# One change in four parts to a fused attention and two-layer kernel: where a rounding runs, how input splits are queued, how fast operands are fetched, how long one weight group is prepared

## The chip, the cores and the metric

The kernel runs on one core of a Trainium2 chip. The metric is the device time of one execution in microseconds. The engines are named as in the profile: PE is TensorE (PEld its weight loads), DVE is VectorE, ACT is ScalarE, POOL is GpSimd, and SP is SyncE, which here issues nearly all the DMAs. Each engine runs its own instructions strictly in the order in which the program emitted them, so an instruction that waits holds up everything behind it on that engine.

## The reference, cut to what matters

```python
def phi(x):                                   # w_phi: 64 x 128
    proj = x @ w_phi
    proj = proj - max(abs(proj))              # over the features
    return concat([exp(proj), exp(-proj)])
num, den = phi(q) @ (phi(k).T @ v), phi(q) @ sum(phi(k))
x = num / (den + 1e-6)                        # 4 batches, 8 heads, 576 tokens, 64 wide
x = x as 2304 tokens x 512
h = x @ w_in;   g = h / (1 + exp(-h));  x = g @ w_out    # 512 -> 2048 -> 512
h = x @ w2_in;  g = h * cos(h);         out = g @ w2_out # 512 -> 2048 -> 512
```

The four weight matrices arrive as 64-bit floats. Products are made to nearly full fp32 accuracy by splitting every operand into a rounded high part and a remainder (hi and lo) and adding three products of parts.

## The kernel before, in words

Attention comes first and ends at about 200 us of the profile. Then come the two layers, and the change lies almost wholly there.

**Blocks, groups and steps.** The 2304 tokens are four blocks of 512 (0 to 3) and a small rest ("S"). The 2048 inner features are four groups g = 0 to 3 of 512. A step treats one block with one group: `step` computes h by a Strassen-like scheme of seven products (p 1 to 7, at L778, each against one of seven weight operands A11, S1, A12, S2, S4, S3, A22), applies the nonlinearity (`act`), and multiplies by w_out (`y`, L844 to L851, with four further weight operands 0 to 3). For each layer the order is: groups 0 to 3 over blocks 0, 1, S, and then groups 0 to 3 again over blocks 2 and 3. A step has seven calls of `fill()` (a small step has four), and each call adds one to a counter, `weights.now`. One such unit is about 3 us of PE work. All hand-made scheduling is in these units: `at[layer, g, block]` is the unit at which a step starts.

**The nonlinearity of the second layer** (`act`) is h * cos(h), in pieces of 128x512. Each piece passes through three stages that `begin` and `advance` emit at fixed places of a step: ACT computes the angle in turns, a = h / 2pi + 1/4 (L811). Then `turns`: DVE rounds a to the nearest integer by adding and subtracting 12582912 in one tensor_scalar (L802), DVE subtracts (L803), ACT takes the sine (L804). Then `times`: three DVE instructions multiply by h and split into gh and gl (L807 to L809). A full step has four such pieces; there are 72 in all. In a step, ACT also makes the copies of product banks at L959, L965 and L973, for which PE waits before it goes on with those banks.

**Input splits** (`Inputs.build`). Before a block can be used, its four quarter blocks and four differences T1 to T4 are split into hi and lo: `split` puts ACT's copy to hi (L613) and DVE's subtraction for lo (L614) next to each other as one task. Blocks that come back from memory are read by four load tasks of two DMAs each (L598) into the places where the lo parts will lie, so a lo may be written only when the differences that read that raw block are done. The differences of these blocks run on POOL (L607). Each list of tasks is spread over a stretch of units.

**Weight operands.** `in_tasks` and `out_tasks` turn 64-bit weights into fp32 with ACT (L169) and DVE (L170, L175, L181), add them on POOL (L235), and split them on ACT and POOL (L189, L192). All operands are also stored to memory, and from the step (0, 3, 1) on they are fetched again when needed (L131). For the groups of the second layer, the (1, g), this preparation runs ahead and only stores. There are 16 slots of 512 KB, 11 of which a group uses. `fill()` runs `loads()`, which fetches the next wanted operands as long as slots are free; while preparation tasks are left it keeps two slots (SPARE) back. If a step needs an operand that was not fetched, `need` forces it at that place.

Of the kernel before, what the change touches and what calls it, by code (L numbers as in the profile page):

```python
# [7 lines left out]
F32 = mybir.dt.float32  # L8
F32R = mybir.dt.float32r
I32 = mybir.dt.int32  # L10
AF = mybir.ActivationFunctionType
ALU = mybir.AluOpType
# [3 lines left out]
P = 128  # L16
# [17 lines left out]
PB, T2, KN = 2, 2, 2  # L34
# [5 lines left out]
MAGIC = 12582912.0  # L40
INV2PI = 1.0 / (2.0 * math.pi)
# [3 lines left out]
SMALL = "S"  # L45
# [29 lines left out]
class Weights:  # L75
# [53 lines left out]
    def load(self, l, g, n):  # L129
        t = self.slot()  # L130
        self.nc.sync.dma_start(t.bitcast(F32), self.dram[l, g, n])  # L131
        self.have[l, g, n] = t
# [53 lines left out]
    def split(self, t, hi, lo):  # L186
        nc = self.nc
        if self.fast:
            nc.scalar.copy(hi, t)  # L189
        else:  # L190
            nc.gpsimd.tensor_scalar(hi, t, 1.0, 0.0, op0=ALU.mult, op1=ALU.add)
        nc.gpsimd.tensor_sub(lo, t, hi.bitcast(F32))  # L192
# [375 lines left out]
class Inputs:  # L568
# [11 lines left out]
    def build(self, tag, temps, dram=None):  # L580

        nc, i = self.nc, tag[1] % 2
        o = self.ops[i]
        tmp = {}
        where = {"11": 0, "12": 1, "21": 2, "22": 3}

        def block(n):
            kh, th = int(n[0]) - 1, int(n[1]) - 1
            if dram is None:
                return self.xa[:, NJ * i + 2 * th:NJ * i + 2 * th + 2, 2 * kh:2 * kh + 2, :].rearrange("p i c n -> p c i n")  # L590
            return o[:, 1, where[n]].bitcast(F32).rearrange("p c (i n) -> p c i n", n=P)

        def load(n):
            def go():
                kh, th = int(n[0]) - 1, int(n[1]) - 1
                src = dram.rearrange("p (i c n) -> p c i n", i=NJ, c=NC)[:, 2 * kh:2 * kh + 2, 2 * th:2 * th + 2, :]
                for c in range(2):
                    nc.sync.dma_start(block(n)[:, c], src[:, c])  # L598
            return go

        def part(n):
            return tmp[n].rearrange("p (c i n) -> p c i n", c=2, i=2) if n[0] == "T" else block(n)

        def diff(n, a, b, engine):
            def go():
                tmp[n] = temps()
                engine.tensor_sub(part(n), part(a), part(b))  # L607
            return go

        def split(n, idx):  # L610
            def go():
                hi, lo = (o[:, x, idx].rearrange("p c (i n) -> p c i n", n=P) for x in range(2))
                nc.scalar.copy(hi, part(n))  # L613
                nc.vector.tensor_sub(lo, part(n), hi.bitcast(F32))  # L614
                tmp.pop(n, None)
                self.done.add((tag, idx))
            return go

        d, g = nc.vector if dram is None else nc.gpsimd, nc.gpsimd
        out = [] if dram is None else [load(n) for n in ("11", "21", "22", "12")]  # L620
        t1 = diff("T1", "12", "11", d)
        if out:
            after(out[-1], 3, t1)
        return out + [t1, split("11", 0), diff("T2", "22", "T1", d), split("T1", 4),
                      diff("T4", "21", "T2", g), split("21", 2), split("T2", 5), diff("T3", "22", "12", g),
                      split("22", 3), split("T3", 6), split("T4", 1)]

    def build_small(self, tag, temps):
        nc = self.nc
# [22 lines left out]
def after(other, lag, f):  # L652

    f.after = (other, lag)
    return f
# [53 lines left out]
def moe(tc, xa, xd, yd, inputs, norm, norm_pool, weights, tasks, out):  # L709
    nc = tc.nc  # L710
    with ExitStack() as ctx:
        sp = ctx.enter_context(tc.tile_pool(name="mo", bufs=1, side="right", reuse_waits="tile"))
# [3 lines left out]
        inputs.add(sp, 1)  # L716
        quarter = sp.tile([P, 1], F32, name="quarter")
        nc.gpsimd.memset(quarter, 0.25)

        def temps():  # L720
            return weights.pool.tile([P, 2 * TH], F32, name="tt", bufs=2)
# [5 lines left out]
        at = {}  # L727
        n = 0
# [13 lines left out]
        def loads(forced=False):  # L742
            least = 0 if forced or not (tasks.streams.get("in") or tasks.streams.get("out")) else SPARE
            while wanted and opened[0]:
                key = wanted[0]
                if forced:
                    if key in weights.have or key not in weights.saved or not weights.free:
                        return
                    weights.load(*key)
                else:  # L750
                    if key in weights.have or weights.now < weights.saved.get(key, 1e9) + 2 or weights.slots() <= least:
                        return
                    weights.load(*key)
                wanted.pop(0)

        def need(l, g, n):
            key = (l, g, n)
# [31 lines left out]
        def act(s, part, at, h):  # L789

            hi, lo = (t[:, :, at] for t in tile_g(s, part))
            a = sp.tile([P, 2, TH], F32, name="ta", bufs=2)
            if s[0] == 0:
                def silu():
                    nc.scalar.activation(a, h, AF.Silu)
                    nc.scalar.copy(hi, a)  # L796

                return [silu, lambda: nc.vector.tensor_sub(lo, a, hi.bitcast(F32))]  # L798
            b = sp.tile([P, 2, TH], F32, name="tb", bufs=2)

            def turns():
                nc.vector.tensor_scalar(b, a, MAGIC, MAGIC, op0=ALU.add, op1=ALU.subtract)  # L802
                nc.vector.tensor_sub(b, a, b)  # L803
                nc.scalar.activation(b, b, AF.Sin, scale=2.0 * math.pi)  # L804

            def times():
                nc.vector.tensor_mul(b, b, h)  # L807
                nc.vector.tensor_copy(hi, b)  # L808
                nc.vector.tensor_sub(lo, b, hi.bitcast(F32))  # L809

            return [lambda: nc.scalar.activation(a, h, AF.Identity, bias=quarter, scale=INV2PI), turns, times]  # L811

        late = []

# [206 lines left out]
        def queue(l, g):  # L1021
            for kind, q in weights.order.items():
                q.extend((kind, l, GF * g + c) for c in range(GF))

        def plan():
            w = weights
            for l, g in [(0, g) for g in range(1, NG)] + [(1, g) for g in range(NG)]:
                ins, outs = w.in_tasks(l, g, (l, g) not in STORED), w.out_tasks(l, g, (l, g) not in STORED)
                queue(l, g)
                if (l, g) in STORED:  # L1030
                    a, b = at[0, NG - 1, 0] + 2, at[0, NG - 1, 3] + 2
                    ends = (a + (b - a) * g / 3, a + (b - a) * (g + 1) / 3) if g < 3 else (at[1, 0, SMALL], at[1, 2, 0])
                    tasks.add("in", ins, *ends)
                    tasks.add("out", outs, *ends)
                    continue
                b0, b1, bs, nx = at[l, g - 1, 0], at[l, g - 1, 1], at[l, g - 1, SMALL], at[l, g, 0]
                tasks.add("in", ins[:12], *((b0 + 1, b1 - 1) if (l, g) != (0, 1) else (b0 + 6, b1 + 3)))
                tasks.add("in", ins[12:21], b1 - 1, b1 + 6)
                tasks.add("in", ins[21:], b1 + 6, bs + 3)
                tasks.add("out", outs[:3], b1, b1 + 6)  # L1040
                tasks.add("out", outs[3:], bs + 1, nx + 6.5)
            b = inputs.build((0, 1), temps)
            tasks.add("build1", b[:2], 0, 0)
            tasks.add("build1", b[2:], 3, 7)
            l = NG - 1
            for tag, src, used, start in (((0, 2), xd[2], at[0, l, 0], at[0, l, 1] + 2),
                                               ((0, 3), xd[3], at[0, l, 1], at[0, l, SMALL] + 2),
                                               ((1, 0), yd[0], at[0, l, 2], at[0, l, 3] + 1),
                                               ((1, 1), yd[1], at[0, l, 3], at[1, 0, 0]),
                                               ((1, 2), yd[2], at[1, l, 0], at[1, l, 1] + 2),  # L1050
                                               ((1, 3), yd[3], at[1, l, 1], at[1, l, SMALL] + 2)):
                b = inputs.build(tag, temps, src)
                name = f"build{tag[1] % 2}"
                for f, d in zip(b, (1, 3, 4, 6)):
                    tasks.add(name, [f], used + d, used + d)
                tasks.add(name, b[4:], start, start + 8)
            for n, t in enumerate((at[0, 0, 1] + 2, at[0, 0, 3])):
                tasks.add("buildS", inputs.build_small((n, SMALL), temps), t, t + 5)

# [10 lines left out]
        for i, s in enumerate(steps):  # L1070
            layer, g, blk, _ = s
# [100 lines left out]
```

## Time and profile before

| what | value |
|---|---|
| time of the runs | 1027.44 us median of 3 (1024.21 to 1027.95) |
| time of the profiled execution | 1014.94 us |
| its span | 1013.2 us |
| mean granted TensorE clock | 0.987 |

The profiled execution is one execution, and it is 12.5 us shorter than the median of the runs. In the views below a time in the span counts from its start; a busy time is followed by the number of instructions as (x36); "idle before" is time that an engine stood still directly ahead of an instruction, with the instruction that ended it behind an arrow. The second layer begins at about 597 us.

### The profile page before, as it was taken

How to read it: one execution, taken by the hardware profiler on the slowest of the kernel's cores; microseconds unless marked ns; L12 is line 12 of the kernel's file. 1: busy time of each engine (PE TensorE's matmuls, PEld its weight loads, DVE VectorE, ACT ScalarE, POOL GpSimd, SP SyncE). 2: the span in 40 equal slices, each digit the busy share in tenths (PEclk: the TensorE clock that was granted, in tenths of full speed). 3: DMA queues.
4: the chain of work that ended last, by engine and by line, in shares of the span. 5: the costliest groups of instructions: out<-in, count | busy, mean ns of one | idle time of the engine just before them, and what ended most of it. 6: DMA issues, size and time to landing. Idle time of an engine off the chain costs nothing.

```text
span 1013.2 us, 16847 instructions
## 1 busy us (share of the span) xinstructions
PE 968.4 (96%) x6503; PEld 868.3 (86%) x6503; DVE 711.7 (70%) x1045; ACT 491.3 (48%) x918; POOL 279.9 (28%) x251
## 2 busy tenths in 40 slices
PE   8899999989999999989999998999899998999998
PEld 8799988878889998978899877888789877888897
DVE  6668787796756656875555558689876877667766
ACT  5666666765654454465544534452332334443331
POOL 2222554464361522740612621014200121000000
PEclk9999999999999999999999999999999999999999
DMA  5455446265754548878788785243635273443302
GB/s 158 141 136 143 115 139 176 67 234 185 254 204 164 202 165 289 307 301 319 279 305 307 265 298 169 105 172 137 240 135 166 84 260 113 147 161 110 126 1 83
DMA packets 97888, 186.46 MB, mean 184 GB/s; under 512 B 30352, under 2 KB 59152, under 8 KB 97040
## 3 DMA queue, kind: packets, MB, share of 16 engines
q1 hardware_dynamic: 97664, 185.25, 53.8%
q8 instruction: 51, 0.84, 0.3%
q14 instruction: 29, 0.24, 0.1%
q10 hardware_dynamic: 144, 0.13, 0.0%
HBM read 128.06 MB, written 57.22 MB: 183 GB/s over the span
## 4 chain that ended last, share of the span: by engine, by line
PE 69%; DVE 14%; ACT 5%; DMA 4%; POOL 4%; issue 3%; SPq 0%; DVEq 0%; ACTq 0%; POOLq 0%
PE h L778 27%; PE y L844 5%; PE y L845 5%; PE y L846 5%; PE y L851 5%; PE y L849 5%; PE y L850 5%; PE kv L473 3%; PE p L393 3%; PE num L499 2%; DVE tb L803 2%; DVE xa L879 2%; DVE gl L809 1%; DVE xo L614 1%; DVE tb L807 1%
## 5 line engine op out<-in xcount | busy, mean ns | idle before, releaser
L778 PEld LDWEIGHTS h<-xo,w 128*128 128x128 f32 x2688 | 331.7, 189 | 28.0 <-ACT h L959 8.7
L778 PE MATMUL h<-xo,w 128*128 128x256 f32 x2688 | 337.4, 282 | 17.3 <-ACT h L959 7.5
L804 ACT ACTIVATE tb<-tb 128x512 f32<-128x512 f32 x72 | 45.5, 632 | 177.6 <-DVE tb L803 177.2
L844 PE MATMUL y<-gh,w 128*128 128x512 f32 (+1 forms) x320 | 120.7, 377 | 4.6 <-DVE xa L879 3.3
L849 PE MATMUL y<-w,gh 128*128 128x512 f32 x288 | 116.0, 403 | 7.4 <-DVE gh L808 6.5
L845 PE MATMUL y<-gl,w 128*128 128x512 f32 (+1 forms) x320 | 119.9, 375 | 0.5 <-DVE gl L798 0.5
L846 PE MATMUL y<-gh,w 128*128 128x512 f32 (+1 forms) x320 | 119.4, 373 | 0.0
L851 PE MATMUL y<-w,gl 128*128 128x512 f32 x288 | 116.3, 404 | 0.9 <-DVE gl L809 0.9
L850 PE MATMUL y<-w,gh 128*128 128x512 f32 x288 | 115.6, 401 | 0.0
L192 POOL TENSOR_TENSOR w<-wt,w 128x512 fp32r<-128x512 f32 x32 | 45.5, 1422 | 207.3 <-ACT w L189 180.4
L798 DVE TENSOR_TENSOR gl<-ta,gh 128x512 fp32r<-128x512 f32 x72 | 64.3, 894 | 53.6 <-ACT gh L796 53.5
L192 POOL TENSOR_TENSOR w<-stage,w 128x512 fp32r<-128x512 f32 x56 | 79.3, 1425 | 66.6 <-ACT w L189 63.1
L879 DVE TENSOR_TENSOR xa<-y,xa 128x512 f32<-128x512 f32 (+1 forms) x114 | 69.7, 654 | 23.6 <-PE y L846 18.9
L844 PEld LDWEIGHTS y<-gh,w 128*128 128x128 f32 x320 | 60.5, 189 | 15.5 <-DVE xa L879 4.4
L849 PEld LDWEIGHTS y<-w,gh 128*128 128x128 f32 x288 | 55.4, 192 | 19.6 <-DVE gh L808 7.9
L846 PEld LDWEIGHTS y<-gh,w 128*128 128x128 f32 x320 | 60.6, 189 | 11.9 <-POOL w L192 0.2
L845 PEld LDWEIGHTS y<-gl,w 128*128 128x128 f32 x320 | 60.6, 189 | 10.4 <-DVE gl L798 0.8
L851 PEld LDWEIGHTS y<-w,gl 128*128 128x128 f32 x288 | 55.3, 192 | 15.4 <-DVE gl L809 2.2
L473 PE MATMUL kv<-va,kp 128*128 128x65 f32 x512 | 64.7, 270 | 0.2 <-ACT kp L415 0.2
L850 PEld LDWEIGHTS y<-w,gh 128*128 128x128 f32 x288 | 55.3, 192 | 10.8
L473 PEld LDWEIGHTS kv<-va,kp 128*128 128x128 f32 x512 | 62.7, 193 | 0.4 <-ACT kp L415 0.4
L802 DVE TENSOR_SCALAR tb<-ta 128x512 f32<-128x512 f32 x72 | 34.0, 472 | 36.6 <-ACT ta L811 36.6
(115 smaller groups left out, 1621.2 us busy)
## 6 DMA issues: line engine op xcount, KB each, us to landing
w<-d SPq DMA_DIRECT2D x48, 512.0 KB, 5.8
raw_in<-in_moe_w_in SPq DMA_DIRECT2D x32, 512.0 KB, 4.6
raw_out<-in_moe_w_out SPq DMA_DIRECT2D x32, 512.0 KB, 4.5
d<-w SPq DMA_DIRECT2D x32, 512.0 KB, 4.3
rb<-rd SPq DMA_DIRECT2D x16, 288.0 KB, 3.7
va<-in_v SPq DMA_DIRECT2D x32, 128.0 KB, 5.2
yd<-xa SPq DMA_DIRECT2D x4, 1024.0 KB, 4.2
xo<-yd SPq DMA_DIRECT2D x32, 128.0 KB, 5.0
```

What stands on the lines that cost most here:

```text
L192: nc.gpsimd.tensor_sub(lo, t, hi.bitcast(F32))
L473: nc.tensor.matmul(ps[:, c, x, :], kp[n, 1 + 2 * p + x][:, c, j, :], va[:, p + 2 * x, j, :], start=False, stop=(x == 1 and j == NJ - 1))
L778: nc.tensor.matmul(dst[:, ab], w[:, a, ab, c * P:(c + 1) * P], o[:, b, idx, c], start=start and n == 1, stop=n == 12, skip_group_check=True)
L798: return [silu, lambda: nc.vector.tensor_sub(lo, a, hi.bitcast(F32))]
L804: nc.scalar.activation(b, b, AF.Sin, scale=2.0 * math.pi)
L844: nc.tensor.matmul(o, w[:, 0, at], hi[:, f, x], stop=False, **st)
L845: nc.tensor.matmul(o, w[:, 0, at], lo[:, f, x], start=False, stop=False)
L846: nc.tensor.matmul(o, w[:, 1, at], hi[:, f, x], start=False, stop=en)
L849: nc.tensor.matmul(o, hi[:, f, at], w[:, 0], stop=False, **st)
L850: nc.tensor.matmul(o, hi[:, f, at], w[:, 1], start=False, stop=False)
L851: nc.tensor.matmul(o, lo[:, f, at], w[:, 0], start=False, stop=en)
L879: nc.vector.tensor_tensor(v, o, v, op=ALU.add)
```

## The change

1. **Rounding of the second layer.** `angle` now emits two ACT instructions: the angle a as before, and b = a + 12582912 (Identity with a bias tile `magic`). `turns` has one DVE instruction, b = (b - 12582912) - a, a scalar_tensor_tensor, in place of two, and ACT takes the sine with the sign turned.
2. **Input splits.** `split` gives two tasks, `high` (ACT) and `low` (DVE), and a low may come at the earliest one unit after its high. The list has 18 tasks behind the loads in place of 11, with the highs ahead of the lows in groups of two. T1 waits four units for the last load in place of three. The tasks behind the loads are spread over seven units in place of eight; for block (0, 1) the stretch ends at unit 8 in place of 7. Block (0, 0) keeps each pair together.
3. **Fetches.** A call of `loads` that is not forced returns after one fetch.
4. **The group (1, 3)** is prepared over the units at[1, 0, S] to at[1, 2, S] in place of at[1, 0, S] to at[1, 2, 0], which is 36 units in place of 22.

```diff
         def split(n, idx):
...
+            def high():
                 nc.scalar.copy(hi, part(n))
+
+            def low():
                 nc.vector.tensor_sub(lo, part(n), hi.bitcast(F32))
                 tmp.pop(n, None)
                 self.done.add((tag, idx))
-            return go
+
+            return high, after(high, 1, low)
...
-        if out:
-            after(out[-1], 3, t1)
-        return out + [t1, split("11", 0), diff("T2", "22", "T1", d), split("T1", 4),
-                      diff("T4", "21", "T2", g), split("21", 2), split("T2", 5), diff("T3", "22", "12", g),
-                      split("22", 3), split("T3", 6), split("T4", 1)]
+        if loads:
+            after(loads[-1], 4, t1)
...
+        return loads + [t1, h0, t2, h4, l0, l4, t4, h2, h5, l2, l5, t3, h3, h6, l3, l6, h1, l1]
...
+        magic = sp.tile([P, 1], F32, name="magic")
+        nc.gpsimd.memset(magic, MAGIC)
...
                 wanted.pop(0)
+                if not forced:
+                    return
...
-                nc.vector.tensor_scalar(b, a, MAGIC, MAGIC, op0=ALU.add, op1=ALU.subtract)
-                nc.vector.tensor_sub(b, a, b)
-                nc.scalar.activation(b, b, AF.Sin, scale=2.0 * math.pi)
+                nc.vector.scalar_tensor_tensor(b, b, MAGIC, a, op0=ALU.subtract, op1=ALU.subtract)
+                nc.scalar.activation(b, b, AF.Sin, scale=-2.0 * math.pi)
...
-            return [lambda: nc.scalar.activation(a, h, AF.Identity, bias=quarter, scale=INV2PI), turns, times]
+            def angle():
+                nc.scalar.activation(a, h, AF.Identity, bias=quarter, scale=INV2PI)
+                nc.scalar.activation(b, a, AF.Identity, bias=magic)
+
+            return [angle, turns, times]
...
-                    ends = (a + (b - a) * g / 3, a + (b - a) * (g + 1) / 3) if g < 3 else (at[1, 0, SMALL], at[1, 2, 0])
+                    ends = (a + (b - a) * g / 3, a + (b - a) * (g + 1) / 3) if g < 3 else (at[1, 0, SMALL], at[1, 2, SMALL])
...
-            tasks.add("build1", b[2:], 3, 7)
+            tasks.add("build1", b[2:], 3, 8)
...
-                tasks.add(name, b[4:], start, start + 8)
+                tasks.add(name, b[4:], start, start + 7)
```

## Rows read from the trace of the kernel before

**Rows 1.** The page: busy time of each engine, with its share of the span.
```profile
PE 968.4 (96%) x6503; PEld 868.3 (86%) x6503; DVE 711.7 (70%) x1045; ACT 491.3 (48%) x918; POOL 279.9 (28%) x251
```
**Rows 2.** Busy time by stretch: length, PE, PEld, DVE, ACT, POOL, clock, DMA share, GB/s.
```profile
380.00:445.00 65.00, 60.00 (x391) 53.87 (x389) 49.98 (x66) 32.67 (x58) 34.28 (x23) 1.00 0.81 288
600.00:630.00 30.00, 23.94 (x138) 21.04 (x137) 22.87 (x37) 11.13 (x20) 5.31 (x4) 0.94 0.52 178
665.00:720.00 55.00, 48.19 (x276) 41.32 (x276) 51.73 (x71) 20.26 (x36) 17.47 (x13) 0.97 0.35 128
720.00:780.00 60.00, 60.00 (x390) 54.48 (x390) 40.38 (x69) 19.74 (x32) 2.55 (x2) 1.00 0.59 202
780.00:865.00 85.00, 78.01 (x465) 67.83 (x464) 66.88 (x106) 30.66 (x52) 11.40 (x8) 0.96 0.48 154
```
**Rows 3.** Waits of PE, 230 to 870 us: total, times, longest.
```profile
PE h L778 <- ACT h L959: 6.9, 4, 2.7
PE y L849 <- DVE gh L808: 6.5, 3, 3.1
```
**Rows 4.** Timeline, 598 to 626 us: start, length, engine, instruction, idle before.
```profile
603.63 1.30 POOL L607 TENSOR_TENSOR tt<-xo 128x512 f32<-128x512 f32 x1 [11.39 <-DMA xo<-yd]
...
604.97 0.69 DVE L614 TENSOR_TENSOR xo<-xo 128x512 fp32r<-128x512 f32 x1 [3.56 <-POOL tt L607]
...
608.33 0.63 ACT L804 ACTIVATE tb<-tb 128x512 f32<-128x512 f32 x1 [7.06 <-DVE tb L803]
...
609.00 2.90 PE L778 MATMUL h<-xo,w 128*128 128x256 f32 x12 [3.31 <-ACT tb L804]
...
623.22 2.98 PE L778 MATMUL h<-xo,w 128*128 128x256 f32 x23 [2.74 <-ACT h L959]
```
**Rows 5.** Busy time in two 2 us stretches behind stalls of PE.
```profile
610.00:612.00 2.00, 2.00 (x10) 2.00 (x10) 1.97 (x5) 0.22 (x1) 0.00 (x0) 0.50 0.00 0
...
828.00:830.00 2.00, 2.00 (x6) 1.61 (x5) 1.54 (x3) 0.40 (x1) 0.00 (x0) 0.50 0.63 234
```
**Rows 6.** DVE's groups, 665 to 720 us: busy, mean ns, idle before.
```profile
L803 DVE TENSOR_TENSOR tb<-ta,tb 128x512 f32<-128x512 f32 x9 | 6.2, 692 | 0.3
L802 DVE TENSOR_SCALAR tb<-ta 128x512 f32<-128x512 f32 x9 | 5.9, 660 | 0.0
...
L175 DVE SCALAR_TENSOR_TENSOR wt<-raw_out,wt 128x512 int32<-128x512 int32 x3 | 4.3, 1418 | 0.0
...
L181 DVE SCALAR_TENSOR_TENSOR wt<-ws,wt 128x512 int32<-128x512 int32 x3 | 2.1, 684 | 0.0
```
**Rows 7.** DVE's busy time, 665 to 720 us, on tile wt, then on tile stage.
```profile
665.00:720.00 55.00, 7.57 (x9) 0.97 0.35 128
...
665.00:720.00 55.00, 3.58 (x6) 0.97 0.35 128
```
**Rows 8.** The page's costliest groups, by form, whole span: ACT's angle from SBUF.
```profile
L811 ACT ACTIVATE ta<-u,quarter 128x512 f32<-128x512 f32 x32 | 23.1, 723 | 19.3 <-DVE u L979 12.1 <-DVE u L992 7.1
```
**Rows 9.** SP's timeline, 520 to 600 us: DMA issues near the end of layer one.
```profile
591.86 1.59 SPq L131 DMA_DIRECT2D w<-d  x3
593.95 1.72 SPq L598 DMA_DIRECT2D xo<-yd  x2
```
**Rows 10.** DVE's groups, 780 to 865 us.
```profile
L802 DVE TENSOR_SCALAR tb<-ta 128x512 f32<-128x512 f32 x14 | 7.2, 512 | 1.7 <-ACT ta L811 1.7
...
L614 DVE TENSOR_TENSOR xo<-tt,xo 128x512 fp32r<-128x512 f32 x8 | 5.5, 688 | 6.4 <-ACT xo L613 6.4
...
L614 DVE TENSOR_TENSOR xo<-xo 128x512 fp32r<-128x512 f32 x6 | 4.1, 688 | 3.8 <-ACT xo L613 3.8
```
**Rows 11.** DVE's groups, 380 to 445 us.
```profile
L614 DVE TENSOR_TENSOR xo<-xo 128x512 fp32r<-128x512 f32 x6 | 6.9, 1154 | 5.2 <-issue 2.1 <-POOL stage L235 1.9 <-POOL tt L607 1.2
...
L614 DVE TENSOR_TENSOR xo<-tt,xo 128x512 fp32r<-128x512 f32 x7 | 6.2, 893 | 2.9 <-ACT xo L613 2.9
```
**Rows 12.** The page's DMA issues: KB each, median us from issue to landing.
```profile
w<-d SPq DMA_DIRECT2D x48, 512.0 KB, 5.8
```

More of the change, by code (lines that the diff above doesn't have):

```diff
@@ L610, in split @@
         def split(n, idx):
-            def go():
-                hi, lo = (o[:, x, idx].rearrange("p c (i n) -> p c i n", n=P) for x in range(2))
+            hi, lo = (o[:, x, idx].rearrange("p c (i n) -> p c i n", n=P) for x in range(2))
+            def high():
                 nc.scalar.copy(hi, part(n))
+            def low():
                 nc.vector.tensor_sub(lo, part(n), hi.bitcast(F32))
@@ L616, in go, with both @@
                 self.done.add((tag, idx))
-            return go
+            return high, after(high, 1, low)
         d, g = nc.vector if dram is None else nc.gpsimd, nc.gpsimd
-        out = [] if dram is None else [load(n) for n in ("11", "21", "22", "12")]
-        t1 = diff("T1", "12", "11", d)
-        if out:
-            after(out[-1], 3, t1)
-        return out + [t1, split("11", 0), diff("T2", "22", "T1", d), split("T1", 4),
-                      diff("T4", "21", "T2", g), split("21", 2), split("T2", 5), diff("T3", "22", "12", g),
-                      split("22", 3), split("T3", 6), split("T4", 1)]
+        loads = [] if dram is None else [load(n) for n in ("11", "21", "22", "12")]
+        t1, t2, t4, t3 = diff("T1", "12", "11", d), diff("T2", "22", "T1", d), diff("T4", "21", "T2", g), diff("T3", "22", "12", g)
+        if loads:
+            after(loads[-1], 4, t1)
+        h0, l0 = split("11", 0)
+        h4, l4 = split("T1", 4)
+        h2, l2 = split("21", 2)
+        h5, l5 = split("T2", 5)
+        h3, l3 = split("22", 3)
+        h6, l6 = split("T3", 6)
+        h1, l1 = split("T4", 1)
+        if dram is None and tag[1] == 0:
+            def both(*fs):
+                return lambda: [f() for f in fs]
+            return [t1, both(h0, l0), t2, both(h4, l4), t4, both(h2, l2), both(h5, l5), t3, both(h3, l3), both(h6, l6), both(h1, l1)]
+        return loads + [t1, h0, t2, h4, l0, l4, t4, h2, h5, l2, l5, t3, h3, h6, l3, l6, h1, l1]
     def build_small(self, tag, temps):
```

## The prediction

> **What bounds the kernel now.** I read the busy times first: PE is busy for 968.4 of 1013.2 us, so 44.8 us is all that better feeding of PE can return, besides what a slower clock costs [rows 1]. Next I cut the span into stretches. Attention and its hand-over, before 230 us, are hardly touched by the change. From 380 to 445 us PE is idle for 5.0 us. In the second layer the idle time lies in three stretches: 6.1 us (600 to 630), 6.8 us (665 to 720) and 7.0 us (780 to 865), 19.9 us together; between the last two lies one without any [rows 2]. The reader is to compare DVE's column: 51.7 us of 55 in the worst stretch, where the PE work alone takes 48.2, against 40.4 of 60 in the stretch without idle time. DVE is the bound there for a while, though it is busy for only 70% of the whole span. ACT has 20.3 of 55.
>
> The waits say the same: PE waits most for ACT's bank copy L959 and for DVE's gh [rows 3]. The timeline shows how the first comes about. POOL stands 11.4 us for a transfer into xo; DVE, in its own order, stands 3.6 us behind POOL at the low part of a split; the rounding behind that is late, so ACT stands 7.1 us at its sine; and PE stands 3.3 us. Another 2.7 us follow at 620 us, on L959 [rows 4]. So ACT's lateness is DVE's lateness passed on.
>
> A stall costs more than itself. At 610 and at 828 us, just behind stalls, the granted clock is 0.50, the lower level of 1.2 GHz, with PE busy throughout, so each of these 2 us windows loses 1 us [rows 5]. The window rows hold two such dips; the means of 0.94, 0.97 and 0.96 in the three stretches of 30, 55 and 85 us come to 1.8, 1.7 and 3.4 us of missing clock, some 6 us as an estimate, since a mean over a stretch also counts its idle part [rows 2].
>
> **The change part by part.** The sum is made against the profiled execution, 1014.9 us (its span and 1.7 us around it). The median of the runs is 12.5 us more; I take the same saving off it.
>
> *Rounding.* DVE loses L802 and its L803 becomes a scalar_tensor_tensor. There is no fp32 one in the trace; the int32 ones of the same shape take 0.68 us where POOL leaves them alone and 1.42 us in the worst group, and L803 takes 0.69 [rows 6]. I take 0.69, since it too reads two SBUF tensors; the upper end, 1.42, would make the change useless on DVE in crowded places, but rows of that length stand beside POOL's work, which the old pair met as well. So DVE saves 9 times 0.66 = 5.9 us in the worst stretch and 14 times 0.51 = 7.2 us in the last [rows 6, 10]. ACT gains an instruction a piece. The nearest row, an angle from SBUF with a bias tile, is 0.72 us [rows 8], so 72 of them are 52 us on ACT, 9 of them 6.5 us in the worst stretch, where ACT then has 26.8 of 55 [rows 2]. Behind each stand the bank copies and the next sines; the cover is ACT's idle half. Each piece's own way from angle to sine becomes 0.72 - 0.66 = 0.06 to 0.72 - 0.51 = 0.21 us longer; only the last piece of the kernel has no work over it, which is 0.2 us.
>
> A rule of the Trainium skill speaks against this part: "ScalarE: Activation LUTs", section Rules for kernel authors, puts adds on VectorE and not on ScalarE, because the former is faster. The rows agree on the price (0.72 against 0.51 to 0.66). By that rule alone the sum would be 72 times 0.06 to 0.21, or 4 to 15 us more; by the busy columns the slower engine is the free one, and I go by these.
>
> *Longer stretch for group (1, 3).* Its preparation costs DVE 7.6 + 3.6 = 11.2 us in the worst stretch [rows 7]. Spread over 36 units in place of 22, about 0.39 of it, 4.4 us, moves to later, much of it to the stretch with 20 us of DVE free. With the rounding, DVE's need there falls from 51.7 to 41.4 us, below the 48.2 of PE. I take 5.5 of the 6.8 us idle and 1.3 of clock. If the stretch stayed crowded, 3 in place of 6.8.
>
> *Input splits.* In the last stretch DVE stands 6.4 + 3.8 = 10.2 us for ACT's copies at L614 [rows 10], because the two tasks are neighbours. A unit of about 3 us between them covers a copy of 0.6 us, so that wait goes, together with the 7.2 us of L802. What is late next is ACT: a high may follow its difference sooner than before, and then ACT stands for POOL, with L959 behind it. I take 5 of the 7.0 us and 2.4 of clock. At 600 to 630 us the low that waited 3.6 us comes two units later (one for T1, one for the lag), so the first stall, 3.3 us, goes with its clock dip of about 1.5; of the second, 2.7, I take 1.3, since POOL's difference and the denser list still meet DVE there. From 380 to 445 us L614 stands 5.2 + 2.9 us, of which only the 2.9 waits for ACT [rows 11], the list becomes denser, and POOL is busy for half of the stretch; I take 1.5 of 5.0, and the bounds are a loss of 2 and the whole 5.
>
> *Fetches.* Nearly all of SP's bursts are fetches let go together: three at 591.9 us stand ahead of the last two loads of a split [rows 9]. One at a time these loads are issued up to 1.5 us sooner. A group of two full steps has 14 fills for 11 fetches, so the limit fits; but fetches that catch up after a wait for slots are now spread over several units. The work that hides it is the five spare slots and about six units from a slot's release to the next use. Without that cover, a fetch lands 5.8 us after its issue [rows 12]. I charge 3.8 us for late fetches, for ACT behind POOL, and for the longer hold on the two reserved slots during (1, 3); the ends are 0 and 12 (two late fetches at 5.8).
>
> Sum: rounding and stretch 6.8, last stretch 7.4, first stretch 6.1, layer one 1.5, less 3.8 and 0.2: 17.8 us. The profiled execution would take about 997 us, and the runs about 1009.6; I say 1010.
>
> **The rivals.**
>
> *A: DVE is relieved, but ACT behind POOL takes the place of the wait.* For it: POOL's 11.4 us wait for a transfer stays a wait, and h4 follows T1 directly [rows 4]. Against it: T1 comes a unit later. Then only the worst stretch (6.8) and part of the last (3) return, less 2: 7.8 us, about 1020.
>
> *B: nothing that can be told.* Stalls move to other places of these steps: the gains of 21.8 are met by losses of 17 or more. For it: PE is at 96% already. Time 1023 to 1032.
>
> *C: slower, by late operands.* Place: the change from one group to the next, with fetches limited to one a fill and two slots held back until the end of (1, 3). Each group that starts with an operand on its way costs 5.8 us and a clock dip of 1.5, so 7.3 us. There are 12 group changes with fetching. Against it: PE waits for no fetch anywhere in the waits that I read, and the limit is above the mean need. It decides from 17.8 / 7.3, that is from three late groups: these give 1009.6 + 21.9 = 1031.5, and four 1038.8. I name 1036.
>
> *D: the skill's rule.* ACT's longer angle stands ahead of the copies for which PE waits; if each of the 72 pieces delays PE by the 0.21 us, and the three crowded stretches give back nothing, the time is 1027 + 15 - 6 = 1036 (the 6 is the layer-one and split part that does not need DVE).
>
> **Chances.** Forecast (999 to 1017) 0.54; still better than it 0.04; A 0.19; B 0.11; C 0.08; D 0.04. The range from 999 to 1025 holds the forecast, A and part of B, about 8 in 10. The likeliest case alone has 999 to 1017. What a measurement of this kernel can tell from no change is about 0.5%, 5 us: below 1022.3 is faster (forecast, the better case, and most of A: 0.74), 1022.3 to 1032.6 the same (B and the rest of A: 0.14), above that slower (0.12).
>
> **What would show it.** L802 gone, and a second ACT group of 72 with about 0.72 us; the new DVE instruction at 0.69 us; DVE at about 675 us over the span; from 665 to 720 us DVE near 41 of 55 with PE idle under 2 us; L614 with almost no idle time from ACT; no stall at 605 us; fewer dips to 0.50; fetches apart on SP, and none that PE waits for. Wrong it would be if PE's waits named a fetch, if L613 stood long for POOL with L959 behind it, or if the new DVE instruction took over 1 us everywhere.

## The result and the profile after

The changed kernel takes 989.7 us (median of 4 runs, 987.59 to 996.61) against 1025.83 us (median of 4, 1016.5 to 1027.95): ratio 0.968, interval 0.960 to 0.975. It is faster, as forecast, but the time lies below the range of 999 to 1025, and the saving, 36 us, is twice the 17.8 us forecast. Side by side with the kernel before on two chips in later runs, it had ratios of 0.973 (0.969 to 0.976; 990.95 against 1017.1 us) and 0.975 (0.972 to 0.979; 992.18 against 1018.22 us). So the change itself is worth some 26 us; the other 10 us of the first figure come from the executions that were compared there, mostly those of the kernel before (1025.83 us, where later runs have 1016 to 1020).

The page's busy times answer to [rows 1]: the span is 985.8 us, 27.4 less.

```profile
PE 959.2 (97%) x6503; PEld 864.4 (88%) x6503; DVE 672.2 (68%) x973; ACT 542.7 (55%) x990; POOL 278.8 (28%) x252
```

PE stands idle for 26.6 us (44.8 before), and its busy time is 9.2 us shorter with the same 6503 instructions: that part goes with the clock, whose mean over the span is 0.998 against 0.987 before. Busy time by stretch, columns as in [rows 2], with the stretches laid about where the five stages A to E of the table below now lie, so they are not of the same length as before:

```profile
395.00:450.00 55.00, 53.70 (x358) 48.86 (x357) 49.17 (x59) 32.16 (x58) 33.70 (x22) 1.00 0.88 303
590.00:620.00 30.00, 29.01 (x185) 26.05 (x184) 22.96 (x37) 18.44 (x30) 6.07 (x4) 1.00 0.73 263
...
652.00:700.00 48.00, 48.00 (x296) 42.83 (x295) 39.25 (x63) 24.72 (x40) 7.74 (x5) 1.00 0.39 140
700.00:730.00 30.00, 26.91 (x169) 24.57 (x168) 21.61 (x29) 16.80 (x27) 8.40 (x6) 0.94 0.44 164
...
760.00:835.00 75.00, 74.86 (x477) 67.15 (x476) 57.86 (x89) 42.14 (x68) 10.88 (x8) 1.00 0.59 200
```

Four crowded stretches have almost no idle time left, and there the clock is full. One new stall stands in the fourth line, with the only dip of the clock in the second layer. The groups by form over the whole span show the new instructions, L820 on DVE and L830 on ACT; L617 is the old L614, over the whole span:

```profile
L820 DVE SCALAR_TENSOR_TENSOR tb<-tb,ta 128x512 f32<-128x512 f32 x72 | 52.2, 725 | 56.4 <-ACT tb L830 56.4
L830 ACT ACTIVATE tb<-ta,magic 128x512 f32<-128x512 f32 x72 | 52.2, 724 | 2.3
...
L617 DVE TENSOR_TENSOR xo<-tt,xo 128x512 fp32r<-128x512 f32 x32 | 25.0, 786 | 2.2 <-ACT xo L614 2.2
```

**Where the time came from.** The spans of single executions differ, so I compare work and not clock time: ACT's first instruction of each of the 144 pieces of both layers (it writes the tile ta; L795 and L811 before, L813 and L829 after) is a mark, counted from 1, and the same mark stands for the same work. Marks 104 and 117, the stretch from 780 us, in the timeline of ACT, before:

```profile
780.45 0.73 ACT L811 ACTIVATE ta<-u,quarter 128x512 f32<-128x512 f32 x1 [1.06 <-DVE u L979]
...
860.26 0.69 ACT L811 ACTIVATE ta<-h,quarter 128x512 f32<-128x512 f32 x1 [1.34 <-PE h L778]
```

and after:

```profile
763.74 0.72 ACT L829 ACTIVATE ta<-u,quarter 128x512 f32<-128x512 f32 x1 [0.81 <-DVE u L1000]
...
832.87 0.69 ACT L829 ACTIVATE ta<-h,quarter 128x512 f32<-128x512 f32 x1 [1.22 <-PE h L796]
```

that is 79.8 us before and 69.1 us after, a saving of 10.7. The table holds such differences to the kernel before, in us, from each kernel's own profiled execution; the stages are marks 37 to 45 (A, 396 to 448 us of the kernel before), 74 to 77 (B, 600 to 625), 84 to 93 (C, 664 to 723), 93 to 98 (D, 723 to 745) and 104 to 117 (E, 780 to 860). "All" runs from mark 37 to the last. A loss or gain "by stages" below is the difference of two figures of this table, most often to the changed kernel's.

| kernel | A | B | C | D | E | all | ratio of times, interval |
|---|---|---|---|---|---|---|---|
| changed | -3.8 | -6.8 | -9.5 | +5.0 | -10.7 | -26.2 | 0.968 (0.960 to 0.975) |
| changed, e7 | -3.8 | -6.8 | -9.5 | +5.0 | -10.6 | -26.0 | 0.973 (0.969 to 0.976) |
| changed, e15 | -3.8 | -6.8 | -9.5 | +5.0 | -10.7 | -26.1 | 0.975 (0.972 to 0.979) |
| e1 rounding undone | -3.7 | -3.0 | -8.1 | +6.5 | -8.2 | -16.6 | 0.986 (0.981 to 0.990) |
| e2 splits undone | -0.2 | -6.4 | -9.5 | +3.4 | -5.9 | -18.6 | 0.988 (0.982 to 0.993) |
| e3 single fetch undone | -3.8 | -4.7 | -9.5 | +3.4 | -10.6 | -25.0 | 0.975 (0.970 to 0.979) |
| e4 stretch undone | -3.8 | -6.8 | -6.6 | +0.1 | -10.5 | -28.3 | 0.976 (0.972 to 0.981) |
| e5 rounding alone | 0.0 | -3.7 | -4.2 | 0.0 | -6.1 | -14.2 | 0.986 (0.983 to 0.989) |
| e6 splits alone | -3.7 | -2.3 | +0.3 | 0.0 | -7.6 | -12.1 | 0.990 (0.986 to 0.993) |
| e8 (1, 3) from earlier | -3.8 | -6.8 | -5.3 | 0.0 | -11.0 | -27.2 | 0.975 (0.972 to 0.979) |
| e9 spare DVE work behind | -3.8 | -5.2 | -9.2 | +5.3 | -9.8 | -21.8 | 0.977 (0.971 to 0.983) |
| e10 pairs kept | -1.0 | -3.8 | -9.6 | +4.9 | -3.9 | -12.0 | 0.987 (0.980 to 0.994) |
| e11 (1, 3) in two places | -3.8 | -6.8 | -8.5 | 0.0 | -10.6 | -30.2 | 0.968 (0.963 to 0.973) |
| e12 spare ACT work | -3.8 | -6.8 | -9.8 | +2.2 | -10.5 | -28.8 | 0.971 (0.965 to 0.976) |
| e13 spare DVE work ahead | -3.8 | -4.7 | -8.7 | +5.7 | -8.5 | -19.1 | 0.981 (0.977 to 0.986) |
| e14, as e11 | -3.8 | -6.8 | -8.5 | 0.0 | -10.6 | -30.1 | 0.971 (0.967 to 0.974) |

The changed kernel's own three profiles agree to 0.1 us in each stage, so the stages tell more than the times. What differs between executions lies ahead of mark 37: the three profiles take 394.3, 405.0 and 397.9 us to get there. In e7's profile, busy time by stretch shows why, a clock of 0.59 over 25 us at the end of attention, where the change does nothing; the second line is the same stretch in the first profile of the changed kernel:

```profile
175.00:200.00 25.00, 23.30 (x126) 22.71 (x127) 12.22 (x20) 11.57 (x25) 8.49 (x10) 0.59 0.18 48
...
175.00:200.00 25.00, 21.89 (x171) 19.97 (x171) 20.07 (x29) 16.46 (x38) 10.98 (x13) 1.00 0.21 61
```

Medians and stages need not agree where such dips fall into some runs. They differ most for e2: 13 to 15 us lost by its ratio against the changed kernel's, 7.6 by stages. Two of its four runs have mean clocks of 0.979 and 0.986, and ahead of mark 37 its profile (399.4 us) is like those with the splits (e3 397.4, e4 398.6), so I go by the stages; how much of the rest is the change is open.

### The profile page after: what moved, and what is told of

Its sections match the earlier page's. It is cut to its first block, busy times and chain, and to the rows that moved or that the text cites. A ratio compares the mean times of both kernels' runs of the same rounds, so it can differ in the third digit from the quotient of the medians.

```text
span 985.8 us, 16779 instructions
## 1 busy us (share of the span) xinstructions
PE 959.2 (97%) x6503; PEld 864.4 (88%) x6503; DVE 672.2 (68%) x973; ACT 542.7 (55%) x990; POOL 278.8 (28%) x252
## 4 chain that ended last, share of the span: by engine, by line
PE 81%; DVE 7%; ACT 4%; POOL 3%; DMA 3%; issue 2%; SPq 0%; DVEq 0%; ACTq 0%; POOLq 0%
PE h L796 32%; PE y L872 6%; PE y L871 6%; PE y L870 6%; PE y L865 5%; PE y L867 5%; PE y L866 5%; PE kv L473 3%; PE p L393 3%; PE num L499 3%; DVE xo L617 1%; DMA den<-xn 1%; PE t L423 1%; PE num L503 1%; POOL w L192 1%
## 5 line engine op out<-in xcount | busy, mean ns | idle before, releaser
L796 PE MATMUL h<-xo,w 128*128 128x256 f32 x2688 | 338.5, 282 | 10.3 <-ACT h L980 5.5
L872 PE MATMUL y<-w,gl 128*128 128x512 f32 x288 | 114.2, 397 | 0.0
L871 PE MATMUL y<-w,gh 128*128 128x512 f32 x288 | 113.8, 395 | 0.0
L870 PE MATMUL y<-w,gh 128*128 128x512 f32 x288 | 113.4, 394 | 0.0
L820 DVE SCALAR_TENSOR_TENSOR tb<-tb,ta 128x512 f32<-128x512 f32 x72 | 52.2, 725 | 56.4 <-ACT tb L830 56.4
L871 PEld LDWEIGHTS y<-w,gh 128*128 128x128 f32 x288 | 54.2, 188 | 10.9
L870 PEld LDWEIGHTS y<-w,gh 128*128 128x128 f32 x288 | 54.1, 188 | 10.6
```

Of the source, the lines that this page charges most:

```text
L796: nc.tensor.matmul(dst[:, ab], w[:, a, ab, c * P:(c + 1) * P], o[:, b, idx, c], start=start and n == 1, stop=n == 12, skip_group_check=True)
L820: nc.vector.scalar_tensor_tensor(b, b, MAGIC, a, op0=ALU.subtract, op1=ALU.subtract)
L870: nc.tensor.matmul(o, hi[:, f, at], w[:, 0], stop=False, **st)
L871: nc.tensor.matmul(o, hi[:, f, at], w[:, 1], start=False, stop=False)
L872: nc.tensor.matmul(o, lo[:, f, at], w[:, 0], start=False, stop=en)
```

## The experiments

**One part undone at a time** (e1 to e4). e1 takes `turns` and `angle` back to the old two DVE instructions; e2 takes `split`, its list, T1's three units and the old stretches back; the others are one line each.

```diff
 e1 +              nc.vector.tensor_scalar(b, a, MAGIC, MAGIC, op0=ALU.add, op1=ALU.subtract)
    +              nc.vector.tensor_sub(b, a, b)
    -              nc.vector.scalar_tensor_tensor(b, b, MAGIC, a, ...)
 e3 -                if not forced:
    -                    return
 e4 -  else (at[1, 0, SMALL], at[1, 2, SMALL])
    +  else (at[1, 0, SMALL], at[1, 2, 0])
```

> The changed kernel with the rounding back on DVE alone (splits, fetches and stretch stay changed). Theory V (DVE's busy time in the crowded steps of layer two is what PE waited for): DVE is back at 706 us, and PE idles again from about 600 to 620 us and above all while group (1, 3) is prepared; 1000 to 1008 us, ratio to the kernel before 0.975 to 0.985. Theory O (the order of the split tasks is what mattered): within 4 us of the changed kernel, ratio about 0.968 to 0.971.

Measured: 1001.77 us, 9.6 us lost by stages. PE's wait for ACT's bank copy (L980 in the changed kernel, L975 in e1's lines) is back; waits of PE from 590 us on in e1 (4.1 us in two waits in the changed kernel):

```profile
PE h L794 <- ACT h L975: 9.8, 5, 3.8
```

Theory V is right in kind, and PE idles again in B (3.8 us lost) and E (2.5); but C, which it named above all, loses only 1.4 us, and D 1.5. With the longer stretch, DVE probably had room in C even so.

> The changed kernel with the input splits as neighbouring pairs again. Theory V: the rounding has made enough room, so only the 3.8 us of layer one and a few us at 820 us return; 994 to 998 us, ratio 0.971 to 0.976. Theory O: all of the gains at 400, 600 to 625 and 800 to 860 us are lost, 3.8 + 6.8 + 10: 1005 to 1011 us, ratio 0.98 to 0.986. DVE again stands some 10 us for ACT's copies at the low parts.

Measured: 1002.4 us, 7.6 us lost by stages: 3.6 in A, 4.8 in E and 0.4 in B, less 1.6 in D. The median lies between the two theories' times, but the places are V's: B keeps its gain without the splits, which theory O ruled out. In E DVE stands for ACT's copies again (its groups, 770 to 850 us of e2):

```profile
L614 DVE TENSOR_TENSOR xo<-tt,xo 128x512 fp32r<-128x512 f32 x8 | 5.5, 690 | 6.9 <-ACT xo L613 6.9
```

> The changed kernel with fetches let go together again. Theories V and O both: no difference that can be measured (within 4 us, ratio 0.965 to 0.972). Theory F (bursts of fetches delay the loads of the blocks, and with them POOL and DVE): 995 to 1000 us, with POOL's wait for the loads near 600 us back at 11 us from 5.6 us.

Measured: 991.45 us; 1.2 us lost by stages. The mechanism of F is there: POOL's wait for the same loads is 10.73 us in e3's timeline, and 5.59 in the changed kernel's:

```profile
600.11 1.30 POOL L607 TENSOR_TENSOR tt<-xo 128x512 f32<-128x512 f32 x1 [10.73 <-DMA xo<-yd]
```
```profile
592.49 1.29 POOL L607 TENSOR_TENSOR tt<-xo 128x512 f32<-128x512 f32 x1 [5.59 <-DMA xo<-yd]
```

It costs 2.1 us in B, of which D gives most back, so F's size falls. PE waits for no fetch of weights from 590 us on either way.

> The changed kernel with group (1, 3) prepared over 22 units again. The stall of 3.1 us and the clock dip at 718 to 727 us go (4.9 us gained), since no preparation runs beside the first step of group 2 any more; against that DVE has 4.4 us more in the 40 us before. Theory V: the room made by the rounding is enough for that, so the sum is a gain of 0 to 4 us: 986 to 990 us, ratio 0.963 to 0.968. Rival S (the stretch carried a good part of the gain): stalls at 665 to 700 us return, 994 to 998 us.

Measured: 991.89 us; by stages 2.1 us gained, as theory V said (its ratio, 0.976, can't be told from the changed kernel's). D's 5.0 go and C loses 2.9. So by stages the longer stretch, undone last, is a loss. The changed kernel's timeline shows how D's stall comes about:

```profile
715.07 1.29 POOL L192 TENSOR_TENSOR w<-stage,w 128x512 fp32r<-128x512 f32 x1 [1.80 <-ACT w L189]
715.24 1.40 DVE L825 CAST gh<-tb 128x512 fp32r<-128x512 f32 x1
...
716.31 3.15 POOL L235 TENSOR_TENSOR stage<-stage 128x512 f32<-128x512 f32 x2
716.67 1.67 DVE L826 TENSOR_TENSOR gl<-tb,gh 128x512 fp32r<-128x512 f32 x1
718.26 1.48 DVE L170 TENSOR_SCALAR wt<-raw_out 128x512 int32<-128x512 int32 x1
719.67 0.68 DVE L820 SCALAR_TENSOR_TENSOR tb<-tb,ta 128x512 f32<-128x512 f32 x1
720.38 0.63 ACT L821 ACTIVATE tb<-tb 128x512 f32<-128x512 f32 x1 [3.47 <-DVE tb L820]
720.91 0.58 ACT L980 COPY h<-h 128x512 f32<-128x512 f32 x1
...
721.55 0.62 PE L796 MATMUL h<-xo,w 128*128 128x256 f32 x3 [3.09 <-ACT h L980]
721.76 0.43 DVE L825 CAST gh<-tb 128x512 fp32r<-128x512 f32 x1
```

It is the old chain: three DVE instructions (L825, L826, L170) run a microsecond longer than alone while POOL prepares the group, the new rounding (L820) comes late, ACT stands 3.5 us at the sine, and the bank copy behind it holds PE for 3.1. Over the whole trace of the changed kernel, L825 takes 0.43 us in the 64 instances that meet no instruction of POOL and 0.98 to 1.41 us in the 8 that do. The Trainium skill, "SBUF — State Buffer", section Who interferes with whom, says that GpSimd and VectorE share a pair of ports by an exclusive lock, the later one blocking fully. The rows agree in the lengths (L825 and L826 0.43 and 0.69 us a few microseconds later, 1.40 and 1.67 here) and in the ends: L825 ends 0.3 us behind the POOL instruction that began before it, L170 0.3 us behind the last one. They show no port. How much the meeting costs depends on small shifts: D is +3.4 in e2 and e3 and +2.2 in e12, where the same preparation runs.

**One part alone** (e5, e6), and the whole beside them (e7).

> The kernel before with the rounding split over ACT and DVE alone. Theory V (DVE's busy time in crowded steps): more than half of the whole gain, 13 to 16 us below the kernel before, with PE's waits from 665 to 720 us down from 6.8 to under 2 us. Theory O (order of the split tasks): under 8 us.

Measured: 1004.23 us, 14.2 us gained by stages, as theory V said; in C, though, only 4.2 of the 9.5, with 2.9 us of PE's waits left there where V said under 2.

> The kernel before with the input splits as separate tasks alone. Theory V: 6 to 10 us below the kernel before (3.8 in layer one, the rest at 605 and 820 to 860 us), and nothing at 665 to 720 us, where there are no splits. Theory O: 14 us or more. If the parts overlap, this and the rounding alone add up to more than the whole; if each needs the other, to less.

Measured: 1007.56 us, 12.1 us by stages (10.7 by ratio), more than V said and less than O. Nothing in C, as V said. The two gains together are 26.3 by stages and 24.8 by ratio (0.0139 + 0.0105 of 1017), about the whole; but that is chance, for stage by stage they do not add up. In E they overlap (6.1 + 7.6 against 10.7); in C they fall short (4.2 - 0.3 against 9.5, or against the 6.6 of e4, which lacks only the longer stretch); and the whole pays 5.0 in D, which neither has. Neither theory was right alone.

> The changed kernel itself, beside the parts on one chip. If the executions of the kernel before differ by the clock of their attention part and the gain is the same for each, then 26 to 28 us below this chip's kernel before, ratio 0.973 and not 0.968.

Measured: 990.95 us, ratio 0.973: as expected.

**A better place for the preparation** (e8, e11).

```diff
 e8  -  else (at[1, 0, SMALL], at[1, 2, SMALL])
     +  else (at[1, 0, 1] + 3, at[1, 2, 0])
 e11 +  else (at[1, 0, SMALL], at[1, 2, 0])
     +  tasks.add("out", outs, *(ends if g < 3 else (at[1, 0, 1] + 3, at[1, 1, 1] + 4)))
```

> The changed kernel with group (1, 3) prepared from unit at[1, 0, 1] + 3 to at[1, 2, 0], that is over 25 units which end where the old stretch ended. Theory V: the steps from 620 to 650 us have 15 us of DVE free and group 2 starts without preparation beside it, so the 4.9 us at 718 us go and nothing comes in their place: 2 to 5 us below the changed kernel. Rival: the splits of block (1, 1) and the preparation meet around 600 us and cost as much.

Measured: 991.5 us. D's stall goes, but C gives 4.2 us back: 1.0 us gained by stages, short of what theory V said. The rival had the size nearly right and the place wrong: B, around 600 us, is unchanged.

> The changed kernel with the input part of group (1, 3) over the old 22 units and its output part earlier, from at[1, 0, 1] + 3 to at[1, 1, 1] + 4, so that nothing is prepared beside the first step of group 2 and less beside the last steps before it. Theory V: the 5.0 us at 718 us go and the 9.5 us before them stay, so 3 to 5 us below the changed kernel in the second layer. If POOL's work beside DVE costs wherever it lies, 0 to 2 us.

Measured: 986.14 us; by stages 4.0 us gained over the changed kernel, as expected, with D's stall gone and 1.0 lost in C. e14 below has it on one chip with the changed kernel.

**What the parts work by** (e9, e10, e12, e13).

```diff
 e9      nc.vector.scalar_tensor_tensor(b, b, MAGIC, a, ...)
    +    nc.vector.tensor_scalar(spare, a, 1.0, 0.0, op0=ALU.mult, op1=ALU.add)
 e13     (the same line directly ahead of it)
 e12     nc.scalar.activation(b, a, AF.Identity, bias=magic)
    +    nc.scalar.activation(spare, a, AF.Identity, bias=magic)
 e10     return loads + [t1, both(h0, l0), t2, both(h4, l4), t4, both(h2, l2), both(h5, l5), ...]
```

> The changed kernel with one DVE instruction more a piece: a tensor_scalar of 128x512 from ta into a spare tile that nobody reads, behind the new rounding instruction. The sine does not wait for it. Theory V (DVE's time is the price): DVE is back at about 706 us and the time is that of the kernel with the rounding undone, 9 to 13 us above the changed kernel, with losses from 590 to 625, 650 to 700 and 780 to 835 us. Rival W (the gain came from the shorter wait of the sine behind DVE, not from DVE's time): within 3 us of the changed kernel.

Measured: 995.94 us, 4.4 us lost by stages: between V and W. DVE is back at 702.9 us busy, yet less than half of e1's loss comes with it.

> The changed kernel with each high and low kept next to each other in one task for all blocks; T1's four units and the shorter stretch stay. Theory D (the distance between ACT's copy and DVE's subtraction is what the splits gave): as with the splits wholly undone, 7 to 13 us above the changed kernel, with DVE standing some 10 us for ACT's copies. Rival T (T1's later start gave it): within 3 us of the changed kernel.

Measured: 1006.14 us, 14.2 us lost by stages: D holds, T falls. Theory D named 7 to 13 us, and some 10 us of DVE's standing for ACT; at the low parts (L617, 230 to 1000 us) DVE stands 7.5 us for ACT and 14.5 for nothing that the profile shows. It is worse than e2, in B and E above all, so the new stretches and T1's later start, with which alone it differs from e2, hurt the pairs; which of the two was not tried. Keeping the pairs together thus costs 7.6 us with the old timing and 14.2 with the new.

> The changed kernel with one ACT instruction more a piece: a second Identity of 0.72 us into a spare tile, 52 us more for ACT. If ACT's idle half covers it, as the prediction held, within 3 us of the changed kernel. If ACT is near its limit in the crowded steps (the rule that adds belong on VectorE), 10 us or more above it, with PE waiting for the bank copies.

Measured: 988.75 us, no loss (2.6 us gained by stages, all of it in D). The spare ACT work is 51.0 us over the span:

```profile
L832 ACT ACTIVATE spare<-ta,magic 128x512 f32<-128x512 f32 x72 | 51.0, 709 | 0.0
```

So rival D, the slower engine as the limit, falls with twice the load that it was named for.

> The changed kernel with the same spare tensor_scalar of DVE as before, now directly ahead of the new rounding instruction, so that the sine comes behind it in DVE's order. Behind it the spare instruction cost 4.4 us over layers one and two; the rounding undone cost 9.6. Theory P (DVE's time and its place ahead of the sine both count): 8 to 11 us above the changed kernel in the stages from 590 us on. Rival Q (only DVE's time counts, and the other half of the rounding's worth lies in POOL, or in ACT's earlier start): 3 to 6 us.

Measured: 999.26 us, 7.1 us lost by stages: between P and Q, nearer P. The same instruction costs 2.7 us more ahead of the sine's input than behind it.

> The version with the input part of group (1, 3) over the old stretch and its output part earlier, again, beside the changed kernel on one chip. By the stages of the trace it is 4 us faster (30.2 against 26.2 below the kernel before): ratio 0.969 to 0.970 where the changed kernel has 0.973. If the clock of the attention part hides it, the same.

Measured: 988.96 us, ratio 0.971 (0.967 to 0.974).

> The changed kernel again beside it: ratio 0.973 as on the other chip, 26 to 28 us below the kernel before, with the same stages to 0.2 us.

Measured: 992.18 us, ratio 0.975 (0.972 to 0.979), a shade above the expected ratio, with the stages as before. By medians e14 is 3.2 us faster and by stages 4.0; the intervals overlap, so it rests on the stages, which both its profiles show alike. It is the fastest version here.

## Why the prediction was off

The direction and the places held, and the chain in which ACT's lateness is DVE's passed on held too. What failed was the base from which the saving was taken, the sizes of the terms, and the cause given for one of them. The forecast of 1010 us is 20.3 us above the measured 989.7: 11.5 of these come from the base, 8.4 from the terms and 0.4 from rounding up.

**The base** is the last step of the sum, "I take the same saving off" the median, 12.5 us above the profiled execution. It is the step that failed most: 1014.9 - 26.2 = 988.7 is within 1 us of what the changed kernel takes, and the runs of 1024 to 1028 us were not this kernel's usual time. On the three chips of the later runs its medians were 1016 to 1020 us, and there the runs of 1024 us and more have mean clocks of 0.977 to 0.979 and those below 1016 us 0.987 to 0.992. That the first runs had a clock like the former is argued from this; their own clocks are not known.

**The terms**, with what the stages show, come to 26.2 and not 17.8 (25.8 in the five stages, 0.4 between them):

- **Layer one (1.5 us): 3.8.** The splits alone bring it (e6, and e2 loses it). I had feared POOL and the denser list; all but 1.3 us of PE's idle time there is gone.
- **First stretch (6.1): 6.8.** The size was right, but by luck. The prediction gave all of it to the splits, and with the splits undone 6.4 of it stays (e2); alone they bring 2.3. The rounding brings 3.7 alone (3.8 when it is undone), and the single fetch, which was counted as a cost, the 2.1 that e3 loses: with it POOL's wait for the loads is 5.1 us shorter, where I had their issue at most 1.5 us sooner.
- **Rounding and longer stretch (6.8): 4.5**, which is 9.5 in C less 5.0 in D. The gain in C was under-rated and the price of the moved work was not seen in its place. I took DVE's free 20 us after 720 us for room; but a mean over a stretch says nothing of the moment when three DVE instructions meet POOL just ahead of a sine. Undone last, the rounding costs 1.4 in C and the longer stretch 2.9, so either leaves most of the room there; the stretch alone was not run. Over all stages the longer stretch, undone last, is a loss of 2.1 us (e4).
- **Last stretch (7.4): 10.7.** All of PE's 7.0 idle us there came back, and the clock with it, where I had kept a rest of 2 us back for ACT behind POOL. The rounding or the splits alone bring more than half (6.1 and 7.6).
- **The charge of 3.8 for late fetches and ACT behind POOL:** neither came. PE waits for no fetch of weights in the changed kernel, ACT stands for POOL at the highs for 2.2 us in all, and e3 shows the single fetch worth 1.2 us and not a cost. Of the terms this one failed most: a charge for rivals that had chances of their own, and ACT behind POOL had already been charged in the last stretch.

Of the rivals, B (stalls that move elsewhere) came true only in stage D and far from its size; A (ACT behind POOL), C (late operands) and D (ACT's rate) did not. In rival D's time, the 6 us for the layer-one and split part is no term of the sum, where layer one has 1.5 and the splits' places 6.1 and 7.4. The new DVE instruction is 0.73 us on average (0.69 forecast), ACT's 0.72, DVE's busy time is 672 us, as forecast, and L617's wait for ACT is nearly gone.

**What stays open.** The rounding undone costs 9.6 us; DVE's time, put back in the same place ahead of the sine, costs 7.1, of which 4.4 is there wherever it stands. What the other 2.5 are (ACT's part may start earlier than DVE's could) was not settled.

## What to carry to other kernels

When one in-order engine hands its lateness to the next until PE stands, count the idle time of PE in that place together with its clock dip; here nearly all of it came back once the chain had slack. Do not charge rivals in the sum a second time, and take a saving off the same execution from which it was read. Two instructions on different engines that need each other were better kept a step apart in both queues than next to each other (7.6 us in e2, 14.2 in e10), and work moved to a stretch with free time on average can still strike the one instruction behind which a chain hangs (D). Gains of parts that add up over the whole need not add up in any one place (e5, e6). Compare kernels by marks in the work and not by the span, where executions differ by a clock dip that the change has no part in.

## What was not expected of the hardware

At the end of attention the granted clock fell to a mean of 0.59 over 25 us, most of it at the lower level of 1.2 GHz, in one profile of the changed kernel and not in another, with PE busy 23.3 us there against 21.9 at full clock. Just before, from 172 to 176 us, PE was busy for 2.16 of 4 us where the clock fell and for 2.85 where it did not. The 25 us miss 10.3 us of full clock, as an estimate (25 times 0.41); the two profiles are 10.7 us apart at mark 37 (405.0 against 394.3 us), with a second, smaller dip (0.86 from 225 to 250 us) in the slower one. And 51 us more work for ACT, whose busy time was 543 us, cost nothing, though it sits between PE's bank copies.
